# Row making, row stores, matrix loads and fetches in hops 2 to 7 of a graph transformer kernel

## The chip, the cores and the metric

The kernel runs on 1 core of one Trainium2 chip. A core has a matrix engine (TensorE, "PE" in the profile), a vector engine (VectorE, "DVE"), a scalar engine (ScalarE, "ACT"), a general engine (GpSimd, "POOL") and a queue for DMAs (SyncE, "SP"). ACT and POOL issue DMAs too. The metric is the time of one execution on the device in microseconds, the median of the runs.

## The reference

10,000 nodes with 128 features each, 160,000 edges. Seven times each node takes the sum of its neighbours' features, scaled on both sides. Then an attention over the eight stages of each node follows, and a readout.

```python
N, deg, D = 10000, 16, 128          # E = N * deg edges, src and dst drawn at random
h = x
toks = [x]
for _ in range(7):
    msg = h[src] * deg_inv_sqrt[src, None] * deg_inv_sqrt[dst, None]
    h = _segment_sum(msg, dst, N)
    toks.append(h)
tok = jnp.stack(toks, axis=1)       # (N, 8, D)
# layernorm, q k v, softmax over the 8 tokens, residual, readout: (N, D)
```

## The kernel before

**The hops as matrix products.** Nodes lie in 79 groups of 128. A table in SBUF (`tab`) holds the features of all nodes as two float16 halves of 128 columns each: the first half is the value, the second is what rounding left over. There are two such tables; a hop reads one and writes the other. Hop 1 sorts the edges and builds, for each group of 128 target nodes (a *block*), a set of 0/1 matrices in float8, which it keeps in HBM (`GSd`, 592 KB a block). Hops 2 to 7 only load these matrices (`w`) and use them.

**One block** (`block`, L583) does four things.

- *Gather* (`gather`, L624): nine pairs, each of eight small matmuls (L630), pick source rows out of `tab` into one PSUM bank `p` of 128x512. Six banks take turns. Then ACT or VectorE copies the bank to SBUF as float16 (`eb`, L633); the function `evac` says which of the two. Before, ACT has pairs 0, 2, 4, 5, 7 and VectorE 1, 3, 6, 8.
- *Fetched rows*: edges that don't fit into the gather cells are read from the table's copy in HBM by an indirect DMA that GpSimd issues (`fetch`, L558), one from `tabh` (the last groups alone) and one from `tabd` (the whole table) a block. They enter the sum by two matmuls (L594). `ahead` (L776) asks for the fetch of block n + 2 while block n runs. In a block that isn't the first of a hop, the fetch from `tabh` is held: GpSimd first copies a part of an evicted pair into the tile that the fetch will fill (L562), so the fetch can't be issued before that pair has been emptied.
- *Scatter* (`scat`, L603): a matmul of 128x128 for each of 18 groups of cells (L608) adds the gathered rows to the block's sum `acc` in PSUM. It lags by two pairs: the last two pairs of a block are scattered in the next block, after its gathers, and then the block is closed.
- *Finish* (`finish`, L578): VectorE adds the two halves of the sum to `s` (L580). `next_rows` (L657) makes the rows of the next table: ACT the first half (L659), VectorE the second (L660) and the largest magnitude (L661); then ACT issues the store of the rows to HBM (`rows`, L161 to L166), a second store to `tabh` for the first six blocks of a hop. `token_out` (L664) has GpSimd scale `s` (L669) and SP store it (L671). Hop 7 makes no rows.

**Order.** The code is a program for the Tile framework. A planner in it orders the instructions of each engine by their place in the program and by when it expects them to be ready, and sets the semaphores. So an instruction can run ahead of its place in the program where its inputs and a free buffer are there. Each engine and each queue then works strictly in that order. A hop goes through its blocks as 72 to 77, 0 to 71. The rows of a hop's last block are needed by the last gathers of the next hop's first block, and the first fetch from `tabd` needs all rows in HBM. Before, a block's matrices are asked for in program order just ahead of the block (L788, L789), into five buffers; a fetched tile has three buffers (L738).

The copies into tiles and the eviction, as before:

```python
(A.copy if evac(jj) else V.tensor_copy)(e[:, :n, 0:256], p[:, :n]...)     # L633
if jj == 1 and not first and not mid:                                     # L640
    ahead(self.ebuf[(self.eb_i - 1) % len(self.ebuf)][:, 0, 0:128])
```

Of the kernel before, what the change touches and what calls it, by code (L numbers as in the profile page):

```python
# [10 lines left out]
F8 = mybir.dt.float8e4  # L11
I32 = mybir.dt.int32
AF = mybir.ActivationFunctionType
ALU = mybir.AluOpType
# [6 lines left out]
NG = 18  # L21
# [8 lines left out]
NJ = NG + NI  # L30
# [4 lines left out]
NW = NT - 1  # L35
# [5 lines left out]
class Hops:  # L41
# [516 lines left out]
    def fetch(self, t, i, src, name=None, after=None):  # L558

        o = self.ogp.tile([128, 256], F16, name=name or f"og{i}", bufs=2 if name else None)  # L560
        if after is not None:
            self.nc.gpsimd.tensor_copy(o[:, 0:128], after)  # L562
        self.nc.gpsimd.indirect_dma_start(out=o, out_offset=None, in_=src[0] if i == NI else src[1],  # L563
                                          in_offset=bass.IndirectOffsetOnAxis(ap=self.oidx[:, t, i:i + 1], axis=0))
        return o
# [17 lines left out]
    def block(self, t, w, tab, og, pend, lag, runs, first, evac, fin, lead=False, late=False, mid=None, ahead=None):  # L583

        nc, V, A, T, G = self.nc, self.nc.vector, self.nc.scalar, self.nc.tensor, self.nc.gpsimd
        m = 257 if first else 256
        acc = []


        def fetched(i, start=False, stop=False):
            W = w[:, (NG + i) * 128:(NG + i + 1) * 128] if i < NI else self.Sov[:, t, :]
            T.matmul(acc[0][:, :256], W, og[i], start=start, stop=stop)  # L594
            if first:
                T.matmul(acc[0][:, 256:257], W, self.ones16, start=False, stop=False)

        def begin():
            acc.append(self.pacc.tile([128, 512], F32, name="acc", tag="acc"))
            for i in range(NI if late else NI + 1):  # L600
                fetched(i, start=i == 0)

        def scat(e, jj):  # L603
            if not acc:
                acc.append(self.pacc.tile([128, 512], F32, name="acc", tag="acc"))
            for j in range(e.shape[1]):
                J = 2 * jj + j
                T.matmul(acc[0][:, :m], w[:, J * 128:(J + 1) * 128], e[:, j, :m], start=first and J == 0,  # L608
                         stop=J == NG - 1 and not (first or late))
                if first and J == 0 and not lead:  # L610
                    for i in range(NI):
                        fetched(i)

        def close():
            if first:
                if lead:
                    for i in range(NI):
                        fetched(i)
                T.matmul(acc[0][:, 256:257], self.Sov[:, t, :], self.ones16, start=False, stop=False)
            if first or late:  # L620
                T.matmul(acc[0][:, :256], self.Sov[:, t, :], og[NI], start=False, stop=True)  # L621
            self.finish(t, acc[0], fin)

        def gather(jj):  # L624
            n = min(2, NG - 2 * jj)
            p = self.pg.tile([128, 2, 2, 128], F32, name="p")
            for j in range(n):
                for q in range(4):
                    s = 4 * (2 * jj + j) + q
                    T.matmul(p[32 * q:32 * q + 32, j], w[:, NJ * 128 + s * CAP:NJ * 128 + (s + 1) * CAP], tab[:, s, :], start=True, stop=True)  # L630
            e = self.ebuf[self.eb_i % len(self.ebuf)]
            self.eb_i += 1
            (A.copy if evac(jj) else V.tensor_copy)(e[:, :n, 0:256], p[:, :n].rearrange("p j h d -> p j (h d)"))  # L633
            pend.append(lambda: scat(e[:, :n], jj))

        jj = 0
        for i, n in enumerate(runs):
            for _ in range(n):
                gather(jj)
                if jj == 1 and not first and not mid:  # L640
                    ahead(self.ebuf[(self.eb_i - 1) % len(self.ebuf)][:, 0, 0:128])
                jj += 1
            if mid:
                mid(0)
            if not first:
                begin()
                if mid:
                    ahead()
            while len(pend) > lag:
                pend.pop(0)()  # L650
            if mid:
                mid(1)
            if i == len(runs) - 1:
                pend.append(close)
            yield

    def next_rows(self, t, s, new, c, mx, i):  # L657
        nc, V = self.nc, self.nc.vector
        nc.scalar.activation(new[:, t, 0:128], s, AF.Copy, scale=c[:, t:t + 1])  # L659
        V.scalar_tensor_tensor(new[:, t, 128:256], s, c[:, t:t + 1], new[:, t, 0:128], op0=ALU.mult, op1=ALU.subtract)  # L660
        V.tensor_reduce(mx[:, t:t + 1], new[:, t, 0:128], axis=X, op=ALU.max, apply_absolute_value=True)  # L661
        self.rows(i, new, t, t + 1, nc.scalar)

    def token_out(self, k, t, s, ct):  # L664
        r = self.fp.tile([128, 128], F32, name="r")
# [7 lines left out]
    def run(self, ctx, nhop=K):  # L673
        tc, nc, V, A, T, G = self.tc, self.nc, self.nc.vector, self.nc.scalar, self.nc.tensor, self.nc.gpsimd
        with ExitStack() as c:
# [13 lines left out]

            def fin1(t, s, acc):  # L690
                V.tensor_copy(self.indeg[:, t:t + 1], acc[:, 256:257])
                self.next_rows(t, s, self.tab[1], self.c1[1], self.mx[0], 1)
                self.token_out(1, t, s, self.ctok[0])

            quads = [list(range(a, min(NW, a + 4))) for a in (4 * NG, 4 * NG + 4, *range(0, 4 * NG, 4))]
# [38 lines left out]
        with ExitStack() as c:  # L734
            self.gsp = c.enter_context(tc.tile_pool(name="gs2", bufs=5))
            self.pg = c.enter_context(tc.tile_pool(name="pg2", bufs=6, space=PSUM))
            self.pacc = c.enter_context(tc.tile_pool(name="pc2", bufs=2, space=PSUM))
            self.ogp = c.enter_context(tc.tile_pool(name="og2", bufs=3))  # L738
            self.fp = c.enter_context(tc.tile_pool(name="fp2", bufs=4))
            self.sp = c.enter_context(tc.tile_pool(name="sp2", bufs=2))  # L740
            self.ogt = c.enter_context(tc.tile_pool(name="ogt2", bufs=1)).tile([128, NE, 260], F16, name="ogt")
            self.more_ebufs(c.enter_context(tc.tile_pool(name="eb2", bufs=1)), 9)

            V.tensor_scalar(self.sinv, self.sinv, GAIN, None, op0=ALU.mult)
            pend = []
            for k in range(2, nhop + 1):
                i = k % 2
                tab, new = self.tab[1 - i], self.tab[i]
# [16 lines left out]

                def fin(t, s, acc, k=k, ct=ct, c1=c1, mo=mo, new=new, last=last, i=i):
                    if not last:
                        self.next_rows(t, s, new, c1, mo, i)
                    self.token_out(k, t, s, ct)


                order = [*range(4 * NG, NW), *range(4 * NG)]
                og = [[None] * (NI + 1) for _ in order]


# [9 lines left out]
                ahead(-2)  # L785
                ahead(-1)
                for n, t in enumerate(order):
                    w = self.gsp.tile([128, (NJ + NG) * 128], F8, name="w")  # L788
                    nc.sync.dma_start(w, self.GSd[t])  # L789
                    for _ in self.block(t, w, tab, og[n], pend, 2, (9,), False, lambda jj: jj in (0, 2, 4, 5, 7), fin, n == 0, n < 2,  # L790
                                        scale if n == 0 and not last else None, lambda after=None, n=n: ahead(n, after)):
                        pass
                    if n == 9 + NE:
                        pend.append(lambda fin=fin: self.end_block(False, fin))
# [506 lines left out]
```

## Time and profile before

| what | us |
|---|---|
| median of 3 runs | 4059.69 |
| lowest and highest | 4052.91, 4064.12 |
| the profiled execution | 4104.49 |
| its span, first to last instruction | 4102.7 |
| sorting of edges and first table, up to about | 425 |
| hop 1, with the building of the matrices, about | 425 to 1148 |
| hops 2 to 7, about | 1148 to 3402 |
| attention and readout, about | 3402 to 4103 |

The profile is of one execution with the tracing on, so its own time stands beside its span and is not among the three runs. A row of the line view reads: line, engine, operation, tile written <- tiles read, shapes, how often | busy us and mean ns of one | idle time of the engine before it, and what ended it. A row of the timeline has start and length in us, engine, line, operation, count, and in brackets the idle time before it. The chain of waits goes back from the last instruction to what released each step; "issue" in it is time in which an engine waited for nothing that the profile shows. L numbers are lines of the kernel before.

### The profile page before, as it was taken

To read this page: it belongs to the slowest core of one execution; us is meant where nothing else is said; L and a number is where in the kernel's file an instruction comes from. 1 tells how busy PE (TensorE), PEld (TensorE's weight loads), DVE (VectorE), ACT (ScalarE), POOL (GpSimd) and SP (SyncE) were. 2 spreads that over 40 slices of the span, in tenths; PEclk is the share of its full clock that TensorE was granted. 3 is DMA by queue.
4 is the path that set the end of the run, shared out by engine and by line. 5 is a ranking of instruction groups with operands and counts; after the bars stand their busy time and mean duration, and the time that the engine had idled before them with its cause. 6 is when DMAs were issued, how large, how long until landed. Compare 5 with 4: busy or idle time off the path is not lost.

```text
span 4102.7 us, 162923 instructions
## 1 busy us (share of the span) xinstructions
PE 3758.6 (92%) x69041; PEld 2997.0 (73%) x69041; DVE 3277.1 (80%) x7106; ACT 2616.8 (64%) x6733; POOL 1812.3 (44%) x2348
## 2 busy tenths in 40 slices
PE   4776889999989999999999999999999997999997
PEld 3765666776668777777777777777778886878875
DVE  8998999999867776776777677767766665999998
ACT  6774556666656655665666566656655556888884
POOL 0000334333346655665666566556656662222222
PEclk8998999999999999999999999999999999999998
DMA  3100455555556656665666566656655663222220
GB/s 103 30 2 1 153 166 166 167 162 160 155 162 189 189 180 179 186 187 173 184 189 189 170 189 187 191 169 188 187 170 183 185 186 86 79 75 72 80 75 13
DMA packets 320849, 590.42 MB, mean 144 GB/s; under 512 B 56767, under 2 KB 214685, under 8 KB 314861
## 3 DMA queue, kind: packets, MB, share of 16 engines
q1 hardware_dynamic: 207373, 466.89, 36.3%
q0 software_dynamic: 35616, 73.01, 6.9%
q10 hardware_dynamic: 77120, 40.02, 3.4%
q8 instruction: 541, 8.86, 0.9%
q14 instruction: 199, 1.63, 0.1%
HBM read 451.66 MB, written 128.06 MB: 141 GB/s over the span
## 4 chain that ended last, share of the span: by engine, by line
PE 53%; DVE 26%; issue 7%; ACT 6%; DMA 5%; ACTq 1%; another core or an unknown queue 0%; SPq 0%; POOL 0%; DVEq 0%; POOLq 0%
PE p L630 17%; PE acc L608 14%; ACT eb L633 4%; PE acc L594 4%; DMA rb<-srow 3%; DVE eb L633 3%; PE pv L985 3%; DVE s L580 3%; PE po L996 3%; PE pu L974 3%; DVE tab L660 2%; PE ta L333 2%; DVE w L548 2%; DVE oh L199 2%; DVE mx L661 2%
## 5 line engine op out<-in xcount | busy, mean ns | idle before, releaser
L633 ACT CAST eb<-p 128x512 f16<-128x512 f32 x3026 | 1563.9, 602 | 679.4 <-PE p L630 593.6
L633 DVE CAST eb<-p 128x512 f16<-128x512 f32 x1888 | 1236.9, 687 | 438.7 <-PE p L630 185.8
L630 PE MATMUL p<-tab,w 128*32 128x256 f16 x39312 | 1356.4, 275 | 81.1 <-ACT eb L633 24.6
L608 PE MATMUL acc<-eb,w 128*128 128x256 f16 (+1 forms) x9828 | 1242.3, 274 | 9.5 <-issue 5.5
L630 PEld LDWEIGHTS <-w 128*32 128x32 fp8e4 x39312 | 987.9, 96 | 358.5 <-issue 296.0
L608 PEld LDWEIGHTS <-w 128*128 128x128 fp8e4 x9828 | 939.3, 98 | 195.7 <-issue 82.3
L563 POOL DMA_INDIRECT og<-tabh,oidx x546 | 600.2, 1099 | 636.0 <-DVE vi L444 395.3
L563 POOL DMA_INDIRECT og<-tabd,oidx x534 | 574.7, 1076 | 630.3 <-PE acc L621 331.2
L659 ACT ACTIVATE tab<-s,c 128x128 f16<-128x128 f32 x474 | 190.7, 402 | 372.9 <-DVE eb L633 229.8
L669 POOL TENSOR_SCALAR r<-s,ctok 128x128 f32<-128x128 f32 x474 | 296.8, 626 | 49.9 <-DVE s L580 28.8
L660 DVE SCALAR_TENSOR_TENSOR tab<-s,c,tab 128x128 f16<-128x128 f32 x474 | 166.0, 350 | 185.7 <-issue 144.4
L562 POOL COPY og<-eb 128x128 f16<-128x128 f16 x451 | 129.8, 288 | 396.3 <-DVE eb L633 396.3
L580 DVE TENSOR_REDUCE s<-acc 128x128 f32<-128x256 f32 x553 | 229.9, 416 | 37.3 <-PE acc L608 22.1
L319 ACT ACTIVATE o<-oh,d2s 128x79 f16<-128x79 f16 x800 | 204.6, 373 | 81.0 <-PE ta L333 81.0
L1010 ACT ACTIVATE junk<-x 128x128 f32<-128x128 f32 x625 | 245.1, 394 | 0.0
L1068 POOL TENSOR_TENSOR p<-e,in 128x512 f32<-128x512 f32 (+1 forms) x40 | 40.8, 1020 | 344.3 <-DVE e L1066 344.3
L996 PEld LDWEIGHTS po<-v,pT 128*128 128x128 f32 x1250 | 159.7, 194 | 44.4 <-issue 27.4
L333 PE MATMUL ta<-o,ro 128*128 128x158 f16 x1250 | 120.0, 267 | 77.8 <-DVE ro L329 77.8
L985 PE MATMUL pv<-Wv,xT 128*128 128x131 f32 x1250 | 174.6, 282 | 4.6 <-ACT xT L965 3.6
L333 PEld LDWEIGHTS <-ro 128*128 128x128 f16 x1250 | 114.7, 114 | 82.1 <-DVE ro L329 82.0
L996 PE MATMUL po<-v,pT 128*128 128x128 f32 x1250 | 167.6, 278 | 7.4 <-DVE o L1002 7.4
L985 PEld LDWEIGHTS pv<-Wv,xT 128*128 128x128 f32 x1250 | 151.8, 190 | 21.5 <-issue 8.2
(310 smaller groups left out, 4563.6 us busy)
## 6 DMA issues: line engine op xcount, KB each, us to landing
w<-gsd SPq DMA_DIRECT2D x468, 592.0 KB
gsd<-w SPq DMA_DIRECT2D x78, 592.0 KB
rb<-srow SPq DMA_DIRECT2D x78, 576.0 KB
tok<-r SPq DMA_DIRECT2D x546, 64.0 KB
x<-tok SPq DMA_DIRECT2D x266, 128.0 KB
tabd<-tab ACTq DMA_DIRECT2D x474, 64.0 KB
og<-tabh,oidx POOLq DMA_INDIRECT x546
og<-tabd,oidx POOLq DMA_INDIRECT x534
```

What stands on the lines that cost most here:

```text
L319: A.activation(o[:, j - a, NK:, i], oh[:, j, :, i], AF.Copy, scale=d2s[:, c0:c0 + 1])
L333: T.matmul(ta, ro[:, j - a, :, i], o[:, j - a, :, i], start=j + i == 0, stop=j + i == NP)
L563: self.nc.gpsimd.indirect_dma_start(out=o, out_offset=None, in_=src[0] if i == NI else src[1], in_offset=bass.IndirectOffsetOnAxis(ap=self ...
L580: self.nc.vector.tensor_reduce(s, acc[:, 0:256].rearrange("p (h d) -> p d h", h=2), axis=X, op=ALU.add)
L608: T.matmul(acc[0][:, :m], w[:, J * 128:(J + 1) * 128], e[:, j, :m], start=first and J == 0, stop=J == NG - 1 and not (first or late))
L630: T.matmul(p[32 * q:32 * q + 32, j], w[:, NJ * 128 + s * CAP:NJ * 128 + (s + 1) * CAP], tab[:, s, :], start=True, stop=True)
L633: (A.copy if evac(jj) else V.tensor_copy)(e[:, :n, 0:256], p[:, :n].rearrange("p j h d -> p j (h d)"))
L660: V.scalar_tensor_tensor(new[:, t, 128:256], s, c[:, t:t + 1], new[:, t, 0:128], op0=ALU.mult, op1=ALU.subtract)
L669: self.nc.gpsimd.tensor_scalar(r, s, ct[:, t:t + 1], None, op0=ALU.mult)
L985: T.matmul(p[:, g - a, :], S[i]["xT"][:, g, :], Wv, start=True, stop=True)
L996: T.matmul(p[:, g - a, :], PT[i % 2][:, g, :], S[i]["v"][:, g, :128], start=True, stop=True)
L1010: A.activation(j, S[i]["x"][:, g, :], AF.Square, bias=S[i]["x"][:, g, 0:1], scale=-1.0, accum_out=S[i]["sq"][:, g:g + 1])
```

## The change

Hops 2 to 7 are changed in five places; hop 1 keeps its way, and so does the attention. VectorE makes the first half of the rows too, as a `tensor_scalar`, and SP issues the row stores. ACT empties the pairs 0, 2, 3, 5, 6, 8 and VectorE 1, 4, 7. The matrices are asked for in program order three blocks ahead of their use, across the ends of hops too. A fetched tile has four buffers. The copy that holds a fetch reads the block's first pair instead of its second, and copies one column instead of 128.

```diff
-            self.nc.gpsimd.tensor_copy(o[:, 0:128], after)
+            self.nc.gpsimd.tensor_copy(o[:, 0:1], after)
...
-                if jj == 1 and not first and not mid:
-                    ahead(self.ebuf[(self.eb_i - 1) % len(self.ebuf)][:, 0, 0:128])
+                if jj == 0 and not first and not mid:
+                    ahead(self.ebuf[(self.eb_i - 1) % len(self.ebuf)][:, 0, 0:1])
...
-    def next_rows(self, t, s, new, c, mx, i):
+    def next_rows(self, t, s, new, c, mx, i, eng):
         nc, V = self.nc, self.nc.vector
-        nc.scalar.activation(new[:, t, 0:128], s, AF.Copy, scale=c[:, t:t + 1])
+        if eng is nc.scalar:
+            nc.scalar.activation(new[:, t, 0:128], s, AF.Copy, scale=c[:, t:t + 1])
+        else:
+            V.tensor_scalar(new[:, t, 0:128], s, c[:, t:t + 1], None, op0=ALU.mult)
         V.scalar_tensor_tensor(new[:, t, 128:256], s, c[:, t:t + 1], new[:, t, 0:128], op0=ALU.mult, op1=ALU.subtract)
         V.tensor_reduce(mx[:, t:t + 1], new[:, t, 0:128], axis=X, op=ALU.max, apply_absolute_value=True)
-        self.rows(i, new, t, t + 1, nc.scalar)
+        self.rows(i, new, t, t + 1, eng)
...
-            self.ogp = c.enter_context(tc.tile_pool(name="og2", bufs=3))
+            self.ogp = c.enter_context(tc.tile_pool(name="og2", bufs=4))
...
+            order = [*range(4 * NG, NW), *range(4 * NG)]
+            todo = iter(order * (nhop - 1))
+
+            def load_w():
+                t = next(todo, None)
+                w = None
+                if t is not None:
+                    w = self.gsp.tile([128, (NJ + NG) * 128], F8, name="w")
+                    nc.sync.dma_start(w, self.GSd[t])
+                ws.append(w)
...
-                        self.next_rows(t, s, new, c1, mo, i)
+                        self.next_rows(t, s, new, c1, mo, i, nc.sync)
...
-                    w = self.gsp.tile([128, (NJ + NG) * 128], F8, name="w")
-                    nc.sync.dma_start(w, self.GSd[t])
-                    for _ in self.block(t, w, tab, og[n], pend, 2, (9,), False, lambda jj: jj in (0, 2, 4, 5, 7), fin, n == 0, n < 2,
+                    while len(ws) < 4:
+                        load_w()
+                    for _ in self.block(t, ws.pop(0), tab, og[n], pend, 2, (9,), False, lambda jj: jj % 3 != 1, fin, n == 0, n < 2,
```

More of the change, by code (lines that the diff above doesn't have):

```diff
@@ L691, in fin1 @@
                 V.tensor_copy(self.indeg[:, t:t + 1], acc[:, 256:257])
-                self.next_rows(t, s, self.tab[1], self.c1[1], self.mx[0], 1)
+                self.next_rows(t, s, self.tab[1], self.c1[1], self.mx[0], 1, nc.scalar)
                 self.token_out(1, t, s, self.ctok[0])
@@ L744, in run @@
             V.tensor_scalar(self.sinv, self.sinv, GAIN, None, op0=ALU.mult)
-            pend = []
+            pend, ws = [], []
+            order = [*range(4 * NG, NW), *range(4 * NG)]
[7 more added lines that the diff above has]
+                ws.append(w)
             for k in range(2, nhop + 1):
@@ L767, in fin @@
                     if not last:
-                        self.next_rows(t, s, new, c1, mo, i)
+                        self.next_rows(t, s, new, c1, mo, i, nc.sync)
                     self.token_out(k, t, s, ct)
-                order = [*range(4 * NG, NW), *range(4 * NG)]
                 og = [[None] * (NI + 1) for _ in order]
```

## The prediction

> **What bounds the kernel now.** I read the page first and left its busy shares alone:
>
> ```profile
> PE 3758.6 (92%) x69041; PEld 2997.0 (73%) x69041; DVE 3277.1 (80%) x7106; ACT 2616.8 (64%) x6733; POOL 1812.3 (44%) x2348
> ```
>
> They average four stages, of which the change touches one. So I took the sum `s` (L580), made once a block, and let its rows for hop 6 and hop 7 be the clock; both windows begin at the second block of the hop.
>
> ```profile
> L580 DVE TENSOR_REDUCE s<-acc x78: 411/414/425, 2690.0 to 3044.5; 128x128 f32<-128x256 f32 x78
> L580 DVE TENSOR_REDUCE s<-acc x78: 410/424/426, 3067.0 to 3401.6; 128x128 f32<-128x256 f32 x78
> ```
>
> The same 77 steps take 354.5 us in hop 6 and 334.6 in hop 7. Hop 7 does all that hop 6 does except `next_rows`: no row is made and none is stored. So `next_rows` costs 19.9 us a hop, although it lies on engines that are not full. The chain of waits in the middle of hop 4 says how (start, length, what):
>
> ```profile
> 2003.83 0.41 DVE s L580
> 2004.24 0.47 issue
> 2004.71 0.35 DVE tab L660
> 2005.06 0.21 DVE mx L661
> 2005.27 0.17 ACTq L162
> 2005.44 0.04 issue
> 2005.48 0.59 ACT eb L633
> 2006.07 0.04 issue
> 2006.12 0.89 PE p L630 x24
> 2007.01 0.33 PE acc L594 x2
> 2007.33 0.59 PE acc L608 x4
> 2007.92 0.15 DVE eb L633
> 2008.08 0.45 issue
> ```
>
> These pieces make a ring: they add up to 4.69 us, and at 2008.53 the next `s` begins. The first "issue" of 0.47 is ACT's row half (L659), done while VectorE waits for it. Then ACT issues the store, which waits for VectorE's second half, and only behind that issue can ACT empty the first bank of the next block. Six banks hold gathers, so the seventh gather waits for this first bank: the 24 matmuls after it are gathers 7 to 9. In hop 7 the chain is TensorE alone:
>
> ```profile
> 3302.12 0.32 PE acc L594 x2
> 3302.45 1.97 PE acc L608 x18
> 3304.41 2.11 PE p L630 x72
> ```
>
> That is 4.40 us a block, the work of TensorE without a wait. One block of each kind from the timeline, hop 4 and then hop 7, shows the rest of the mechanism:
>
> ```profile
> 2004.55 2.46 PE L630 MATMUL p<-tab,w 128*32 128x256 f16 x72
> 2005.48 2.54 ACT L633 CAST eb<-p 128x512 f16<-128x512 f32 x5 [0.80 <-PE p L630]
> 2006.54 1.02 POOL L563 DMA_INDIRECT og<-tabh,oidx  x1 [0.27 <-POOL og L562]
> 2007.91 0.69 DVE L633 CAST eb<-p 128x512 f16<-128x512 f32 x1 [0.59 <-PE acc L608]
> ```
>
> ```profile
> 3299.93 2.20 PE L630 MATMUL p<-tab,w 128*32 128x256 f16 x72
> 3300.60 2.54 ACT L633 CAST eb<-p 128x512 f16<-128x512 f32 x5 [1.87 <-PE p L630]
> 3300.70 2.48 DVE L633 CAST eb<-p 128x512 f16<-128x512 f32 x4 [1.33 <-PE p L630]
> 3301.46 0.29 POOL L562 COPY og<-eb 128x128 f16<-128x128 f16 x1 [0.92 <-DVE eb L633]
> 3302.02 1.02 POOL L563 DMA_INDIRECT og<-tabh,oidx  x1 [0.27 <-POOL og L562]
> 3303.33 0.42 DVE L580 TENSOR_REDUCE s<-acc 128x128 f32<-128x256 f32 x1
> 3303.34 0.94 POOL L563 DMA_INDIRECT og<-tabd,oidx  x1 [0.30 <-PE acc L608]
> ```
>
> In hop 4 the gathers end at 2007.01, yet VectorE empties the last bank only at 2007.91; in hop 7 `s` begins at 3303.33. Both are about 0.3 us after GpSimd's first fetch is over (2007.56 and 3303.04): while a fetch is being issued, TensorE's signals seem to come through late. In hop 4 this holds VectorE 0.59 us with `s` queued behind, which closes the ring.
>
> **The change, part by part.** Durations are those of the profiled execution, which took 4104.5 us around a span of 4102.7; the median of the plain runs is 4059.7, 44.8 less. I make the sum against 4104.5 and take 44.8 off at the end.
>
> *Both halves on VectorE, store on SP, ACT with gathers 0, 2, 3, 5, 6, 8.* ACT loses the row half and one or two store issues, and gains one eviction. From hop 7's row, five evictions take 2.54, so about 0.49 apart; six take 3.03. ACT begins 0.67 after the first gather, ends at 3.70 and is wanted again at 4.40 + 0.67 = 5.07: 1.37 free. VectorE loses one eviction of 0.69 and gains the first half. No row of before shows that instruction at this size; the nearest are these two, below it 79 columns with the same kind of scalar, above it a second input:
>
> ```profile
> L764 DVE TENSOR_SCALAR c<-dis,q 128x79 f32<-128x79 f32 x5 | 1.3, 250 | 0.0
> L660 DVE SCALAR_TENSOR_TENSOR tab<-s,c,tab 128x128 f16<-128x128 f32 x474 | 166.0, 350 | 185.7 <-issue 144.4
> ```
>
> Between 0.25 and 0.35 I take 0.30. From `s` on VectorE then runs 0.41 + 0.30 + 0.35 + 0.21 with some 0.03 between, 1.3 in all. With `s` at 3.40 after the first gather as in hop 7 it is done at 4.7, and its first eviction is wanted at 4.40 + 0.77 = 5.17: 0.5 spare. The new ring, `s` to `s` through VectorE, is 1.3, an eviction of 0.69, gathers 8 and 9 (two thirds of 0.89), 0.33, 0.59 and a late signal of 0.15 to 0.60: 3.7 to 4.1, under 4.40. So TensorE's own 4.40 ends last, as in hop 7. Gain: 19.9 us in each of hops 2 to 6, **99.5 us**. If that cover is gone, each tenth of a us that the ring exceeds 4.40 costs 5 x 77 x 0.1 = 38 us.
>
> *SP's queue.* SP now issues a row store (two in the first six blocks) beside a matrix load and a token store, at the 0.32 of L789's row below each: 1.0 to 1.3 of 4.40. The row store waits for VectorE, and behind it stand the token store and the next matrix load. These rows show how much air the loads have:
>
> ```profile
> SPq L789 <- PE acc L608: 1031.3, 414, 5.1
> L789 SPq DMA_DIRECT2D w<-gsd x468: 319/320/654, 1148.3 to 3382.1; - x156
> ```
>
> Loads already wait for a buffer that TensorE frees, 2.5 us each on average, and the last one goes out at 3382.1, 19.5 us or over four blocks before the last `s`. "3 blocks ahead" therefore asks for what the planner did already: price nothing, bounds 0 and 0.
>
> *Fetches.* The copy is of one column instead of 128 and hangs on ACT's first eviction (done at 0.67 + 0.59 = 1.26) instead of VectorE's (0.77 + 0.69 = 1.46), so a fetch starts 0.2 to 0.5 earlier, about 1.6 to 1.9 after the first gather. POOL idles 0.92 a block in hop 7, so its own time is covered. With four buffers instead of three one more token-row fetch fits into the run of fetches at a hop's start, where nothing covers it:
>
> ```profile
> 1526.59 0.42 DVE L580 TENSOR_REDUCE s<-acc 128x128 f32<-128x256 f32 x1 [0.41 <-PE acc L608]
> 1527.86 0.35 DVE L660 SCALAR_TENSOR_TENSOR tab<-s,c,tab 128x128 f16<-128x128 f32 x1
> 1534.09 0.95 POOL L563 DMA_INDIRECT ogl<-tabd,oidx  x1 [0.30 <-issue]
> 1534.76 0.41 PE L630 MATMUL p<-tab,w 128*32 128x256 f16 x6 [0.41 <-issue]
> 1535.34 0.94 POOL L563 DMA_INDIRECT og<-tabd,oidx  x1 [0.30 <-issue]
> ```
>
> Fetches follow each other by 1.25 us there while TensorE runs a handful of matmuls at a time. Bounds 0 and 1.25 a hop; I take 1.25, **6 x 1.25 = 7.5 us lost**. Could the hold gain at a hop's start? Its first block is not held at all in hops 2 to 6, so I expect nothing.
>
> *The last row of a hop*, which the next hop's last gathers need. Before, 1.27 us lie between `s` (1526.59) and the second half (1527.86), since ACT has an eviction in between; after, 0.41 + 0.30 + 0.06 = 0.77. Gain 0.5 x 5 = **2.5 us**. [...]
>
> Sum: 4104.5 - 99.5 - 2.5 + 7.5 = 4010.0; less 44.8, rounded up a little since the plain runs may lose a bit less to the ring, **3966 us**.
>
> **The rivals.** *A part of the gain.* The earlier fetch meets the evictions that feed gathers 7 to 9. Nine gathers take 2.11, so the ninth starts 1.88 after the first, and its bank, ACT's second, is empty at 0.67 + 0.59 + 0.49 = 1.75: 0.13 to spare, and 0.15 to 0.18 for the two before it. A hold of 0.30 would thus cost 0.15 in each of 6 x 77 = 462 blocks: 3966 + 69 = **4035**. For it: signals do come late behind fetches, and the fetch starts about when the third bank is emptied. Against it: the late signals seen are TensorE's, not ACT's.
>
> *Slower.* The same place, the whole hold: the 0.59 that now meets the last eviction falls on evictions 1 to 3, 0.44 a block is left after 0.15 to spare, in all six hops: 3966 + 462 x 0.44 = **4169**. It ends above the time before once the hold is over 0.35, for then more than 94 / 462 = 0.20 a block is lost. It decides if the fetch starts before the third eviction has signalled, under 1.75 after the first gather; I expect 1.6 to 1.9, so this is not remote, but it needs signals from ACT and VectorE to be held like TensorE's, which no row shows. [...]
>
> *It does not do what it says.* The ring is not the rows but the late signal alone; ACT's last eviction takes VectorE's place in it and nothing moves: **4060**. Against it: hop 7 has the late signal and runs at 4.40.
>
> **How the numbers follow.** Forecast 0.76, from 3942 (the extra fetch costs nothing, 7.5, and two or so of the fetches now in the run at a hop's start fall later, 6 x 2.5 = 15) to 3990 (a quarter of the 99.5 stays). A part of the gain 0.11, no change 0.05, slower 0.08. The range reaches from 3942 to 4035: below it lies almost nothing, above it the no-change case, the slower one and the worse end of the partial one. Over 0.3% (12 us, about what a measurement of this kernel tells from no change) faster: 0.76 + 0.11 = 0.87. Within it 0.05, slower 0.08.
>
> **What would show it.** Right: in hops 2 to 6 the chain between two sums is TensorE alone, 4.40 a block; 77 steps of hop 6 take about 335; ACT has no L659 work in them; SP's loads still wait for a buffer. The first six blocks of a hop show it most plainly, at 4.4 to 4.7. Wrong: gathers 7 to 9 stop behind an eviction of ACT or VectorE, hop 7 slower than 334.6, or TensorE waiting for a matrix. A longer run of fetches at the hop starts shows in the time from the last `s` of one hop to the second of the next, 3044.5 to 3067.0 or 22.5 us before.

## The result and the profile after

The kernel after takes 3999.2 us (median of four runs, 3990.6 to 4001.5), beside 4061.9 us (4052.9 to 4069.7) of the kernel before: ratio 0.9842, 95% interval 0.9816 to 0.9869, 62.7 us less. That lies in the range of 3942 to 4035, but 33 us above the forecast and above 3990, the end of the band that had most of the chance (0.76); the stretch from there to 4035 was set aside for a gain that another mechanism cuts down. The profiled execution of after, one of the four runs, took 4001.5 us around a span of 3999.7, where that of before took 4104.5 around 4102.7. So between the two profiles 103.0 us went, where the forecast said 94.5; between the plain runs only 62.7 went. That difference is what most of the explanation is about.

The busy times of the page, then the rows of `s` (L580) for hop 6 and hop 7 from their second block on, as for before:

```profile
PE 3686.7 (92%) x69041; PEld 3006.2 (75%) x69041; DVE 3162.3 (79%) x7033; ACT 2727.3 (68%) x6806; POOL 1763.7 (44%) x2348
```

```profile
L580 DVE TENSOR_REDUCE s<-acc x78: 407/415/426, 2610.1 to 2943.0; 128x128 f32<-128x256 f32 x78
L580 DVE TENSOR_REDUCE s<-acc x78: 414/415/425, 2965.8 to 3298.7; 128x128 f32<-128x256 f32 x78
```

Hop 6 now takes 332.9 us and hop 7 332.8 (354.5 and 334.6 before): making rows costs nothing any more. The chain of waits in the middle of a hop is TensorE alone, 0.32 + 1.97 + 2.08 = 4.37 us a block:

```profile
1990.01 0.32 PE acc L594 x2
1990.33 1.97 PE acc L608 x18
1992.30 2.08 PE p L630 x72
```

One block of hop 4 from the timeline (in after L662 and L663 are the two row halves, L672 is GpSimd's scaling, L162 the row store, L757 the matrix load):

```profile
2003.35 1.02 POOL L563 DMA_INDIRECT og<-tabh,oidx  x1 [0.27 <-POOL og L562]
2004.83 0.69 DVE L633 CAST eb<-p 128x512 f16<-128x512 f32 x1 [0.95 <-PE acc L608]
2005.44 0.41 DVE L580 TENSOR_REDUCE s<-acc 128x128 f32<-128x256 f32 x1
2005.89 0.28 DVE L662 TENSOR_SCALAR tab<-s,c 128x128 f16<-128x128 f32 x1
2006.16 2.15 PE L630 MATMUL p<-tab,w 128*32 128x256 f16 x72
2006.21 0.46 DVE L663 SCALAR_TENSOR_TENSOR tab<-s,c,tab 128x128 f16<-128x128 f32 x1
2006.61 3.25 ACT L633 CAST eb<-p 128x512 f16<-128x512 f32 x6 [1.11 <-PE p L630]
2006.90 1.35 DVE L633 CAST eb<-p 128x512 f16<-128x512 f32 x2
```

The late signal is still there: the fetch ends at 2004.37, and VectorE waits 0.95 us before its last eviction at 2004.83. But ACT begins its six evictions 0.45 us after the first gather whatever VectorE does, so no gather waits for the rows. In 426 of the 462 steps of hops 2 to 7 a block takes at most 4.55 us, in before in 107. Of the other 36 one lies in the same view: in the block that begins at 1996.66 both fetches fall among the gathers, and one gather waits behind an eviction of ACT.

All steps between the sums `s` of the profiled kernels, in us. "Blocks" is the sum over hops 2 to 7 of the time from the second to the last `s` of a hop, "starts" the sum of the six stretches from the last `s` of a hop to the second of the next. Before and after are the two profiles of the result; the rest are the runs below. The last four ran on two chips where the kernel before takes 3937.5 and 3938.6 us. On the first of them TensorE's signals do not come late behind a fetch, as the eviction rows below show; the second is taken to be of its kind by its times alone. On the others, the late chips, they do, and the kernel before takes 4053 to 4070 us.

```
kernel                      blocks   starts   hops 2 to 6, one by one
before                      2107.9   148.9    353.1 355.3 355.7 354.7 354.5
before, once more           2063.1   151.3    337.9 355.1 339.4 342.9 349.9
store alone (late chip)     2028.8   150.0    339.5 337.3 337.9 337.5 337.6
after, old fetches          2037.9   145.6    340.1 339.2 340.9 339.8 339.4
fetches alone               2145.0   161.3    361.6 362.0 362.8 362.6 363.4
after                       1998.4   154.1    333.2 333.3 332.9 333.3 332.9
after, once more            2000.3   154.9    333.1 333.3 334.0 333.9 333.3
before, no fetches          1994.4   129.3    332.1 332.3 332.7 334.0 332.8
after, all fetches held     2128.9   116.4    359.6 353.5 359.2 357.9 361.7
half alone                  1991.7   103.6    332.5 332.3 332.3 332.0 332.0
store alone (first chip)    1985.6    98.5    330.3 331.2 331.6 330.5 331.4
rows (half and store)       1986.1    97.8    330.5 332.5 330.2 331.5 330.9
after, two token buffers    1985.2    94.5    330.5 332.5 330.6 331.3 330.3
```

### The profile page after: what moved, and what is told of

It is laid out like the page before. It is cut to its first block, busy times and chain, and to the rows that moved or that the text cites. A ratio compares the mean times of both kernels' runs of the same rounds, so it can differ in the third digit from the quotient of the medians.

```text
span 3999.7 us, 165770 instructions
## 1 busy us (share of the span) xinstructions
PE 3686.7 (92%) x69041; PEld 3006.2 (75%) x69041; DVE 3162.3 (79%) x7033; ACT 2727.3 (68%) x6806; POOL 1763.7 (44%) x2348
## 4 chain that ended last, share of the span: by engine, by line
PE 72%; DVE 17%; DMA 6%; issue 3%; ACT 1%; SPq 0%; ACTq 0%; POOL 0%; DVEq 0%; another core or an unknown queue 0%; POOLq 0%
PE p L630 25%; PE acc L608 24%; DMA rb<-srow 4%; PE acc L594 4%; PE pv L998 3%; PE po L1009 3%; PE pu L987 3%; PE ta L333 2%; DVE w L548 2%; DVE oh L199 2%; PE pt L977 2%; DVE ro L329 1%; DVE ux L212 1%; DVE R L205 1%; DVE o L205 1%
## 5 line engine op out<-in xcount | busy, mean ns | idle before, releaser
L633 ACT CAST eb<-p 128x512 f16<-128x512 f32 x3494 | 1832.8, 595 | 815.3 <-PE p L630 673.5
L633 DVE CAST eb<-p 128x512 f16<-128x512 f32 x1420 | 962.8, 692 | 591.5 <-PE acc L608 379.6
L630 PE MATMUL p<-tab,w 128*32 128x256 f16 x39312 | 1279.6, 275 | 58.2 <-issue 33.5
L608 PE MATMUL acc<-eb,w 128*128 128x256 f16 (+1 forms) x9828 | 1242.1, 274 | 5.4 <-issue 4.4
L630 PEld LDWEIGHTS <-w 128*32 128x32 fp8e4 x39312 | 991.6, 97 | 256.4 <-issue 214.7
L608 PEld LDWEIGHTS <-w 128*128 128x128 fp8e4 x9828 | 939.5, 98 | 192.0 <-issue 78.8
L672 POOL TENSOR_SCALAR r<-s,ctok 128x128 f32<-128x128 f32 x474 | 296.2, 625 | 74.9 <-DVE s L580 56.5
L580 DVE TENSOR_REDUCE s<-acc 128x128 f32<-128x256 f32 x553 | 230.0, 416 | 50.1 <-PE acc L608 25.9
L663 DVE SCALAR_TENSOR_TENSOR tab<-s,c,tab 128x128 f16<-128x128 f32 x474 | 202.3, 427 | 18.7 <-ACT tab L660 4.8
L562 POOL COPY og<-eb 128x1 f16<-128x1 f16 x451 | 82.9, 184 | 234.2 <-ACT eb L633 234.2
L594 PE MATMUL acc<-og,w 128*128 128x256 f16 x546 | 154.6, 283 | 0.8 <-issue 0.8
```

The source lines that it names most:

```text
L580: self.nc.vector.tensor_reduce(s, acc[:, 0:256].rearrange("p (h d) -> p d h", h=2), axis=X, op=ALU.add)
L672: self.nc.gpsimd.tensor_scalar(r, s, ct[:, t:t + 1], None, op0=ALU.mult)
```

## The experiments

My theory was the prediction's: rows made on ACT and stored by ACT close a ring of 4.69 us a block, with TensorE's late signals behind GpSimd's fetches as one link. Rivals: the ring goes through the held fetch and not through ACT's store; or the fetches matter and the rows do not. The open number was the 44.8 us by which the profile of before lay above its plain runs: either the ring is not closed in all blocks of all executions, or tracing lengthens it.

### The parts of the rows' change, one by one

The first chip got four kernels, each the kernel before with one part of the change in hops 2 to 7. Both halves on VectorE and the store on SP (shortened; hop 1 keeps its way):

```diff
-        nc.scalar.activation(new[:, t, 0:128], s, AF.Copy, scale=c[:, t:t + 1])
+        V.tensor_scalar(new[:, t, 0:128], s, c[:, t:t + 1], None, op0=ALU.mult)
...
-        self.rows(i, new, t, t + 1, nc.scalar)
+        self.rows(i, new, t, t + 1, nc.sync)
```

> The kernel before, with VectorE making the first half and SP storing the rows in hops 2 to 7; evictions, fetches, buffers and matrix loads as before. Theory (the ring: sum, ACT's half, ACT's store issue, ACT's first eviction, gathers 7 to 9): the ring is open, 77 steps of hop 6 take 333 to 337 us, and the time is 55 to 65 us under the kernel before run beside it. Rival (the earlier fetch and the eviction split made the gain): hop 6 stays at 345 to 355 and the time within 15 us of before.

The store alone (the second line of that diff):

> The kernel before, with SP storing the rows; ACT still makes the first half. Theory: without the issue ACT is free right after its half, but VectorE still waits for that half; the ring through VectorE is 0.41 + 0.47 + 0.35 + 0.21 + 0.69 + 0.60 + 0.33 + 0.59 + 0.60 = 4.25 us, just under 4.40: hop 6 at 334 to 340, 45 to 65 us under before. Rival (both halves on VectorE are what counts): under a third of the gain, 0 to 20 us.

The first half alone (the first line):

> The kernel before, with VectorE making the first half; ACT still issues the row store. Theory: ACT's first eviction still stands behind the issue, which waits for VectorE's second half; the ring is shorter by 0.47 - 0.33 = 0.14, 4.55 instead of 4.69: hop 6 at 342 to 350 and about half the gain, 20 to 40 us under before. Rival (the hand-over between VectorE and ACT is the whole cost): the full 60.

The pairs that ACT empties, alone:

```diff
-    lambda jj: jj in (0, 2, 4, 5, 7)
+    lambda jj: jj % 3 != 1
```

> The kernel before, with ACT emptying pairs 0, 2, 3, 5, 6, 8 and VectorE 1, 4, 7, nothing else. Theory: the last eviction, which the late signal holds, leaves VectorE, so the sum no longer stands behind it and the ring loses 0.15 + 0.45: 4.1 to 4.3, open in most blocks; 40 to 60 us under before, less in the first six blocks of a hop, where ACT issues two stores. Rival (ACT's load counts): ACT has 0.49 a block more to do and still the half and the issue, so the time is the same as before or 0 to 30 us above.

Measured against before on that chip, in this order: 0.9956 (0.9940 to 0.9973), 0.9963 (0.9949 to 0.9977), 1.0004 (0.9994 to 1.0013), 0.9982 (0.9972 to 0.9991). That is 15, 12, -2 and 6 us where 55 to 65, 45 to 65, 20 to 40 and 40 to 60 were expected: the theory of each missed, since it counted on a closed ring, and on this chip there was none: the kernel before took 3937.5 us there (20 runs, 3932.8 to 3941.9), 124 less than beside after. The kernel with the half alone takes the same time as before, and its hop 6 runs at TensorE's pace with the rows' store still on ACT:

```profile
L580 DVE TENSOR_REDUCE s<-acc x78: 410/414/425, 2550.5 to 2882.5; 128x128 f32<-128x256 f32 x78
```

What differs shows in VectorE's evictions, here the group of the line view in the middle of hop 4, first the profile of before, then the half alone on this chip:

```profile
L633 DVE CAST eb<-p 128x512 f16<-128x512 f32 x240 | 159.6, 688 | 42.1 <-PE acc L608 31.9 <-PE p L630 5.9
```

```profile
L633 DVE CAST eb<-p 128x512 f16<-128x512 f32 x256 | 159.2, 684 | 40.9 <-PE p L630 40.7
```

On the first, VectorE is let go only after scatters (L608) that come later in TensorE's order than the gather it waits for; on the second by the gather itself (L630). The fetches are as long on both (1016 and 948 ns for the two kinds, 1017 and 950 on this chip). So the late signal differs from chip to chip, and without it the ring does not close. These four runs could not tell the rings apart; what they say is that on such a chip the parts are worth 0 to 0.44%.

### The kernel before once more

No edit, on another chip.

> The kernel before once more, profiled. Theory (the ring closes only in a part of the blocks, and the profiled execution with 4104.5 us held it in nearly all): another profiled execution lies at 4050 to 4075, and fewer steps between sums are over 4.55 us, by about 1 for each 0.3 us that it is shorter. Rival (the profiling itself makes the kernel before 45 us longer): 4100 to 4108 again, with the same steps.

This execution was profiled and took 4063.9 us, within the plain runs on that chip (4046.9 to 4073.8). So tracing does not lengthen the ring. The 4104.5 us of the first profile was a rare execution: of the 27 runs of before on chips with late signals none took more than 4077.1. Its rows for hops 2 and 3:

```profile
L580 DVE TENSOR_REDUCE s<-acc x78: 415/425/426, 1176.2 to 1514.1; 128x128 f32<-128x256 f32 x78
L580 DVE TENSOR_REDUCE s<-acc x78: 412/415/425, 1539.9 to 1895.0; 128x128 f32<-128x256 f32 x78
```

337.9 and 355.1 us with the same instructions: in hop 2 18 of 77 steps are over 4.55 us, in hop 3 66. The steps gather at about 4.4 and 4.7, so the ring has two ways to go, and an execution changes between them. In hops 2 to 6 it was closed (steps over 4.55 us) in 335 of 385 steps of the first profile and in 208 of this one. All blocks together took 2107.9 us and 2063.1, 44.8 less; that this is the very difference between the first profile and the plain median is chance, as the spans differ by 40.6. By their times the plain runs of before are like this second profile, with the ring closed in about half of their blocks; no trace of them was kept.

### The fetches alone, and all but the fetches

The kernel before with the three edits that touch the fetches:

```diff
-            self.nc.gpsimd.tensor_copy(o[:, 0:128], after)
+            self.nc.gpsimd.tensor_copy(o[:, 0:1], after)
...
-                if jj == 1 and not first and not mid:
-                    ahead(self.ebuf[(self.eb_i - 1) % len(self.ebuf)][:, 0, 0:128])
+                if jj == 0 and not first and not mid:
+                    ahead(self.ebuf[(self.eb_i - 1) % len(self.ebuf)][:, 0, 0:1])
...
-            self.ogp = c.enter_context(tc.tile_pool(name="og2", bufs=3))
+            self.ogp = c.enter_context(tc.tile_pool(name="og2", bufs=4))
```

> The kernel before, with the fetch's part of the change alone: held until the block's first pair, a copy of one column, four buffers a fetched tile. Theory: the fetch starts 0.2 to 0.5 us earlier, so the signal that it holds back comes that much earlier and the ring of 4.69 falls to 4.2 to 4.5: a third to all of the interior gain, 20 to 60 us, less 5 at the hop starts for one more fetch in the run. Rival (the fetch has no part in the ring): 0 to 8 us above before.

Measured: 4150.3 us, ratio 1.0233 (1.0196 to 1.0270), 97 us slower, which no theory had. Its hop 6 takes 363.4 us. By the table the blocks lose 82 us and the starts 10 against the kernel before once more.

The chain of waits is the ring of the prediction, link for link, here the part after VectorE's second half:

```profile
1996.64 0.35 DVE tab L660
1996.99 0.21 DVE mx L661
1997.20 0.17 ACTq L162
1997.37 0.04 issue
1997.41 0.59 ACT eb L633
1998.01 0.04 issue
1998.05 0.89 PE p L630 x24
1998.94 0.33 PE acc L594 x2
1999.26 0.67 PE acc L608 x4
```

It goes round in 4.77 instead of 4.69, and it is closed in 358 of the 385 steps of hops 2 to 6, where the kernel before once more had 208. Hop 7 makes no rows, and there the same edit gains: 332.6 us against 338.0. The timeline shows why the hold matters:

```profile
2001.16 1.49 PE L630 MATMUL p<-tab,w 128*32 128x256 f16 x48
2001.90 2.06 DVE L633 CAST eb<-p 128x512 f16<-128x512 f32 x3
2002.18 2.54 ACT L633 CAST eb<-p 128x512 f16<-128x512 f32 x5 [0.81 <-PE p L630]
2002.83 0.18 POOL L562 COPY og<-eb 128x1 f16<-128x1 f16 x1 [1.00 <-ACT eb L633]
2003.29 1.02 POOL L563 DMA_INDIRECT og<-tabh,oidx  x1 [0.27 <-POOL og L562]
```

With the row store still on ACT, ACT's first eviction is the late one (2002.18, VectorE's is at 2001.90). A fetch that hangs on it starts 2.13 us after the first gather, not 1.99 as in before (2006.54 - 2004.55), and the late signal comes later too: 4 scatters take 0.67 instead of 0.59. I had expected the fetch to start earlier.

The other way round, the kernel after with these three edits undone (the same diff, backwards):

> The changed kernel with the fetches as before: held until the second pair, 128 columns copied, three buffers. Theory: the ring stays open without the fetch's part, so the blocks go on at 4.37 to 4.41 (hop 6 at 333 to 336), and a hop's start is shorter by about 1 us: 3 to 8 us under the changed kernel. Rival (the fetch's place is needed): 20 to 60 us above the changed kernel.

Measured: 4031.5 us, ratio 0.9940 (0.9923 to 0.9957), so 22 us less than before where the whole change is worth 62 to 66. The expectation fell: the edit of the fetches, worthless by my sum and harmful alone, is worth some 0.9% once the rows are off ACT. By the table it takes 39.5 us from the blocks and adds 8.5 at the starts. In the blocks of this kernel the first fetch starts 2.21 us after the first gather and the gathers take 2.26 (1.56 and 2.15 in after):

```profile
2000.49 2.26 PE L630 MATMUL p<-tab,w 128*32 128x256 f16 x72
2002.70 1.02 POOL L563 DMA_INDIRECT og<-tabh,oidx  x1 [0.27 <-POOL og L562]
```

The chain of waits there shows TensorE alone, with longer gathers, and a step of 4.48 us. The rows are not the reason: hop 7 of this kernel makes none, its fetch starts 2.19 us after the first gather (the median, as the two that follow), its gathers take 2.24, and it takes 338.4 us, where hops 2 to 6 take 339.2 to 340.9. So a fetch that starts at the end of the gathers costs TensorE some 0.1 us a block on this chip, and one that starts at 1.62, as in hop 7 of the fetches alone, does not (gathers of 2.15). On the first chip the half alone has fetches at 2.06 and gathers of 2.15 all the same. Why the place of the fetch matters is open.

### No fetches

The kernel before, leaving out the fetches of hops 2 to 7 after a hop's start (the first tiles are used again, so the fetched rows are missing from the sums):

```diff
                 def ahead(n, after=None, og=og, order=order, din=din):
+                    if n > 0:
+                        if n + 2 < NW:
+                            og[n + 2] = og[2]
+                        return
+                    if n == 0:
+                        for m in range(NE):
+                            self.fetch_end(m, din[0])
```

> The kernel before, but in hops 2 to 7 only the fetches of a hop's first blocks are issued; later blocks use one fetched tile again and again (the fetched rows of the sums are left out or wrong, all else is computed). Theory (a fetch that is being issued holds TensorE's signals back, and this closes the ring): without fetches the last eviction of a block comes right after its gathers, the ring is under 4.1 and hops 2 to 6 run at 4.37 to 4.41 with ACT still making and storing rows: 77 steps of hop 6 in 333 to 337. Rival (late signals have another cause): hop 6 stays at 350 to 356.

Measured: 3973.8 us in one run, 79 less than before on that chip. With rows and store on ACT as ever, hop 6 takes 332.8 us:

```profile
L580 DVE TENSOR_REDUCE s<-acc x78: 411/415/425, 2585.8 to 2918.6; 128x128 f32<-128x256 f32 x78
```

So the rows do not close the ring by themselves; rows on ACT and fetches together do. (The copies that hold the fetches are left out with them, so the two are not told apart here.) The starts fall by 22 us too (129.3 against 151.3).

### The store alone, on a chip with late signals

> The kernel before, with the row stores of hops 2 to 7 issued by SP instead of ACT and nothing else; once more, because the first chip on which this was tried showed no late TensorE signals (the kernel before ran blocks of 4.37 us there) and so could not tell the rings apart. Ring as predicted (first row half on ACT, the store's issue on ACT, ACT's first eviction, gathers 7 to 9, late signal): without the issue ACT's first eviction comes about 0.25 us earlier, the closed ring shrinks from 4.69 to 4.45 or is open at 4.40, 50 to 70 us less than before in its plain runs, ratio 0.983 to 0.988. Rival, a ring through the held fetch (VectorE's first eviction, copy L562, first fetch, late signal, VectorE's last eviction, the sum s, ACT's half, VectorE's second half and maximum, VectorE's first eviction: 0.75 + 0.56 + 1.02 + 0.33 + 0.61 + 0.44 + 0.44 + 0.51 = 4.66): the store's issue is not in it, closed blocks stay at 4.69 and the ratio is 0.997 to 1.000. On a chip without late signals both expect 0.996.

Measured: 4024.0 us, ratio 0.9895 (0.9869 to 0.9920), 46 us less than before. The rival through the held fetch, which wanted blocks of 4.69, falls. The predicted ring stands, with a gain a little under its 50 to 70: the median step is 4.42. Hops 2 to 6 take 337.3 to 339.5 us and hop 7, without rows, 338.9, so the rows cost nothing any more with the store alone moved. What this kernel has left over the 333 of after goes with the old fetches, not with the rows.

```profile
2001.34 0.43 DVE L580 TENSOR_REDUCE s<-acc 128x128 f32<-128x256 f32 x1 [0.19 <-PE acc L608]
2001.80 0.40 ACT L659 ACTIVATE tab<-s,c 128x128 f16<-128x128 f32 x1 [0.63 <-DVE s L580]
2002.63 0.32 SPq L162 DMA_DIRECT2D tabd<-tab  x1
2003.01 2.54 ACT L633 CAST eb<-p 128x512 f16<-128x512 f32 x5 [0.81 <-PE p L630]
```

ACT still makes the half at once after `s`, but then it waits for the gather (L630) and no longer for its own queue. The link that closed the ring was the store in ACT's queue: its wait for VectorE and its issue, which no run here takes apart.

### The kernel after once more, and with all fetches held

On the same chip as the last:

> The kernel after, unchanged, beside the others on one chip. Where TensorE's signals come late (VectorE waits 0.5 us and more for TensorE behind a fetch), both theories expect the ratio measured first, 0.982 to 0.987, with blocks of 4.37. Where they do not, the ring was never closed before, and only the last row of a hop and the hop starts are left of the change: 10 to 25 us, ratio 0.994 to 0.998.

4004.2 us, ratio 0.9850 (0.9821 to 0.9879): the first result again, on a chip with late signals.

The kernel after, with the fetches of token rows and of the rows at the end held as well:

```diff
-    og[m][NI] = self.fetch(order[m], NI, din, "ogl" if m < 2 else None)
+    og[m][NI] = self.fetch(order[m], NI, din, "ogl" if m < 2 else None, after=after if n else None)
...
-    self.fetch_end(n - 8, din[0])
+    self.fetch_end(n - 8, din[0], after)
...
+    if after is not None:
+        self.nc.gpsimd.tensor_copy(self.ogt[:, k, 0:1], after)
```

> The kernel after, with the fetches of token rows and of the rows at the end also held by the copy of one column (from the second block of a hop on): the run of fetches back to back at a hop's start falls from 10 to 5. If that run is what TensorE waits out there: 5 x 1.25 = 6.3 us less in each of six hops, 37 us less than the kernel after, 25 to 40 in all, blocks still 4.37. Rival: the fetches only move into the first blocks, where TensorE is held by them all the same: the same as the kernel after within 10 us, and blocks 2 to 6 of a hop longer than 4.4. If the second held copy closes a ring through the fetches, blocks go over 4.4 everywhere: 462 x 0.1 = 46 us longer.

4086.6 us, ratio 1.0052 (1.0028 to 1.0075), 82 us slower than after. Both halves of this are telling. At a hop's start GpSimd's run in after goes from the first to the last of these rows, ten fetches 1.25 to 1.3 apart; with all held it is five:

```profile
2590.32 1.01 POOL L563 DMA_INDIRECT ogl<-tabd,oidx  x1 [4.49 <-DMA tok<-r]
...
2601.80 0.96 POOL L568 DMA_INDIRECT ogt<-tabd,oidx  x1 [0.30 <-issue]
```

```profile
2657.31 1.01 POOL L563 DMA_INDIRECT ogl<-tabd,oidx  x1 [4.73 <-DMA tok<-r]
...
2662.61 0.96 POOL L563 DMA_INDIRECT og<-tabd,oidx  x1 [0.30 <-issue]
```

The six starts took 116.4 us, 38.5 less than after's 154.9, where 37 was expected. What TensorE does during such a run, in after (busy us and matmuls in 12 us at a start and 12 us later on):

```profile
2590.00:2602.00 12.00, 7.84 (x88) 0.76 0.20 45
2610.00:2622.00 12.00, 12.00 (x267) 1.00 0.69 195
```

A third of the matmuls gets through. But in the middle of a hop the second fetch now follows the first by 0.30 in each block, and the chain shows the price, 1.57 us for 4 scatters that took 0.59 in before (L596, L610 and L582 are L594, L608 and L580 here):

```profile
1990.16 0.32 PE acc L596 x2
1990.48 1.57 PE acc L610 x4
1992.05 0.02 issue
1992.08 0.44 DVE s L582
```

Two fetches close together hold TensorE's signals much longer (4 scatters of 0.11 are 0.44, so 1.1 late and not 0.15). The scatters themselves go on about 0.11 us apart (in a later block 18 take 2.13 us from 2004.37 on, and the `s` that needs the first four begins at 2006.56), so the signal is late and not the work. Hop 6 goes to 361.7 us. It was the third outcome named, and larger than the 46 us put on it.

### Two buffers for the token rows

The kernel after, to shorten the run at the start without a hold:

```diff
-    og[m][NI] = self.fetch(order[m], NI, din, "ogl" if m < 2 else None)
+    og[m][NI] = self.fetch(order[m], NI, din, "ogl" if m < 2 else "ogn")
```

> The kernel after, with two buffers instead of four for the fetched token rows (tabd) of hops 2 to 7 from the third block on; the held fetches (tabh) keep four, and no hold is added. The run of fetches back to back at a hop's start falls from 10 to 8; in the middle of a hop the second fetch of a block still waits for TensorE to be done with a buffer, once a block. If each fetch of that run costs 1.25 us of TensorE: the six hop starts take 154.5 - 6 x 2.5 = 139.5 us, blocks stay at 4.37 and the interiors at about 1987, so 15 us less than the kernel after: a span near 3986, ratio to the kernel before about 0.981 where TensorE's signals come late. Rival: the two fetches are only put off into blocks 2 and 3, and what the start gains the first blocks lose: 0 to 3 us less, ratio 0.985. If two buffers are too few in the middle of a hop (the second fetch lands after the block that needs it has come to its close), TensorE waits for it and blocks go over 4.37: slower than the kernel after.

3920.7 us, ratio to before 0.9964 (0.9951 to 0.9977), but on the chip where before took 3938.6, by its times one without late signals. Blocks are 4.37 and the starts 94.5 us. Whether it beats the kernel after is left open: after was not run on a chip of this kind, and this kernel was not run on one of the other. Moving the rows alone gave as much on the first chip (ratio 0.9956, starts 97.8), so on such chips a gain of the fetches' edit is not shown.

## Why the prediction was nearly right

**The ring: right.** Hops 2 to 6 were to lose 99.5 us between the profiles and lost 107.7 (1773.3 to 1665.6). Most of the 8 more is hop 7's own: the forecast put all hops at its 334.6, and after runs all at about 333, 5 x 1.5 = 7.5. The path was right as well: taking the store out of ACT's queue opens the ring (store alone, on a late chip), and the fetches are its other condition (no fetches; the first chip). But the 19.9 us a hop, taken from one profile, is not what rows cost in a usual execution: in the kernel before once more hops 2 to 6 take 345.0 us on the mean and hop 7 338.0, so the rows cost 7.0 us a hop there, 35 in all.

**Hop starts: right.** +5.0 forecast (7.5 for the fetch more, 2.5 back for the last row), +5.2 measured between the profiles (148.9 to 154.1), +2.8 against the kernel before once more. The parts are near their sizes: the fetches' edit alone adds 10.0 there, and 8.5 under the moved rows (7.5 forecast); all but the fetches' edit takes 5.7 off (2.5 forecast for the last row).

**The subtraction of 44.8: wrong, the mis-sized term.** The prediction made the sum for the profiled execution, 4010.0 (it came out at 4001.5), and took 44.8 off, as if the plain runs of after would lie as far below its profile as those of before did. It added that "the plain runs may lose a bit less to the ring". In fact the 44.8 was ring time: the profiled execution had the ring closed in most blocks (335 of 385 steps), the plain runs, by their time, in about half. With the ring gone the difference goes too: after's profile lies 2.3 us above the median of its runs. Against the plain runs the ring gives 2063.1 - 1998.4 = 64.7, less some 3 at the starts: 62, as measured (62.7; the two profiles are of different chips). The 44.8 had to come off the gain, not off the sum. Then the forecast would have been 4010.0, 11 us above the measured 3999.2.

**The fetches: wrong, though small in the sum.** "Price nothing" holds for the matrix loads, which wait for a buffer as before. It does not hold for the hold: alone it costs 97 us, and under the moved rows it is worth 39.5 us of blocks. This error and the 44.8 go opposite ways, and the range held the time only because it reached up to 4035 for the rival of a partial gain, whose mechanism did not show. That part is luck. On one chip the store alone gave 46 us of the 66 of the whole change; the other 20 belong to the rest of the change, for which the prediction had no gain in the blocks. It got the gain between the profiles nearly right because hop 7 of the first profile, its yardstick, happened to take 334.6; in the three other profiles of chips with late signals where hop 7 has the old fetches, it takes 338.0 to 338.9 us.

**The first half: right, the second not.** L662 took 0.29 (0.30 forecast). The second half went from 0.35 to 0.45, since it now begins just after GpSimd's scaling (below). From `s` to the end of the rows it is 1.43 instead of 1.3, and in the block shown VectorE's next eviction begins 0.04 us after the rows: the 0.5 us to spare were not there, since `s` came 3.65 us after the first gather and not 3.40. Nothing was lost: the eviction begins 0.74 us after the first gather, as in hop 7 of before (0.77).

**The rivals.** Partial gain and slower needed ACT's and VectorE's signals to be held. The slower one was to decide if the fetch started under 1.75 us after the first gather. It starts at 1.56, yet the gathers take 2.15 and the blocks 4.37, so its condition came true and its mechanism did not show. "No change" said that the late signal alone is the ring: it is a condition, but not the whole.

## What to carry to other kernels

When the profiled execution and the plain runs differ by more than the scatter of the runs, first find which blocks differ: if it is the very stall that the change removes, the difference comes off the gain. Look for an instruction that waits in an engine's queue only to issue a DMA: here the row store held ACT's first eviction and closed a ring of 4.69 us a block, where TensorE's own work is 4.40, through engines that are idle a quarter of the time and more (VectorE 25%, ACT 37% in hop 6 of before); issuing it from SP took 46 us off on a late chip. Check on which engine a held fetch will hang: here the copy moved from VectorE's first eviction to ACT's, the late one in that ring, the fetch started 2.13 us after the first gather instead of 1.99, and with the other two edits of the fetches the kernel took 97 us more. A single profile can also mislead as a yardstick: with the old fetches hop 7 took 334.6 us in the first profile and 338.0 to 338.9 in three others.

## What the runs showed of the hardware

- TensorE's signals come late while GpSimd issues an indirect DMA: in the block of after shown above VectorE waits 0.95 us, until 0.46 us after the fetch has ended, and behind two fetches in a row the signal is 1.1 us late. TensorE gets 88 matmuls through in 12 us instead of 267 during a run of ten.
- This differs between chips, and one kernel shows it on two of them. With the store alone TensorE starts 63 to 79 matmuls during the nine fetches in a row (11.2 us) that open hops 3 to 6 on the late chip, and 161 to 237 on the first; blocks take 2028.8 and 1985.6 us, starts 150.0 and 98.5. In three of the five comparisons with the kernel before it took 4053 to 4070 us, in the other two 3937.5 and 3938.6. Why chips differ is open; nothing here tried it.
- What VectorE's second half and GpSimd's 128x128 scaling cost each other goes by when they begin, not by how long they lie side by side. In after 335 of 395 second halves (L663) begin 0.04 to 0.08 us after the scaling (L672) and take 0.46 us on the mean instead of 0.35, while the scaling stays at 0.62. In before 314 of 395 (L660) begin 0.17 to 0.27 us after it (L669), lie wholly beside it, and both keep their 0.35 and 0.62. In the store alone on the late chip 191 begin about 0.05 us ahead of it: they take 0.36, and the scaling 0.77. One pair of each, in this order:

```profile
2006.14 0.62 POOL L672 TENSOR_SCALAR r<-s,ctok 128x128 f32<-128x128 f32 x1
2006.21 0.46 DVE L663 SCALAR_TENSOR_TENSOR tab<-s,c,tab 128x128 f16<-128x128 f32 x1
```

```profile
2004.50 0.62 POOL L669 TENSOR_SCALAR r<-s,ctok 128x128 f32<-128x128 f32 x1
2004.71 0.35 DVE L660 SCALAR_TENSOR_TENSOR tab<-s,c,tab 128x128 f16<-128x128 f32 x1 [0.47 <-issue]
```

```profile
2002.24 0.36 DVE L660 SCALAR_TENSOR_TENSOR tab<-s,c,tab 128x128 f16<-128x128 f32 x1 [0.47 <-ACT tab L659]
2002.28 0.77 POOL L669 TENSOR_SCALAR r<-s,ctok 128x128 f32<-128x128 f32 x1
```

The first two pairs both lie wholly beside the scaling: in the first the half takes 0.11 us more than in the second. A fetch can delay the second half too: in after with the old fetches 149 of them begin about 0.37 us into a fetch and take 0.50. The new first half takes 0.29 us on the mean in after, whether it meets a fetch (359 of 395) or not, but the three that begin 0.5 us into a fetch from `tabd` take 0.47; in after with the old fetches two, 0.54 and 0.55 us into such a fetch, take 0.46 and 0.45. The fetches from `tabd` that it meets in after take 0.95 us, as in before.
